# Turning a spectrum by TensorE in place of a trip through DRAM, with a new order on the DMA queue, at the start of a DFT and FFN kernel

## The chip, the cores and the metric

The kernel runs on one core of one Trainium2 chip. The metric is the time of one execution in microseconds of device time. Each change is given as a ratio with a 95% interval.

The engines are named as in the profile: PE is TensorE (PEld its weight loads), DVE is VectorE, ACT is ScalarE, POOL is GpSimd, SP issues DMAs. "L377" is line 377 of the kernel in question. The two kernels have different line numbers for the same code: ACT's copies of stage A are L358 before and L377 after.

## The reference

```python
def _attn_ref(x, filt_r, filt_i):            # x: 8 x 3008 x 256
    X = np.fft.rfft(x, axis=1)
    Y = X * (filt_r + 1j * filt_i)[None]
    return np.fft.irfft(Y, n=x.shape[1], axis=1).astype(np.float32)

def _moe_ref(x, w_in, w_out):                # w_in: 256 x 2048, w_out: 2048 x 256
    h = np.maximum(x @ w_in, 0.0)
    return (h * h @ w_out).astype(np.float32)
```

The second function works on the result of the first, for all 24,064 tokens.

## The kernel before

The DFT of length 3008 = 64 x 47 is taken in steps, for each of eight batches. **Stage A** multiplies x by a table over 47 points and gives u. **Stage B** needs u with another index on the partitions; to turn it, u is written to DRAM (`dU`) and read back as `ut`. Stage B multiplies by 24 tables and by the filter F (`prod`), and the stage that it feeds (`unit_p`) begins the inverse and gives `ze`. `ze` makes a trip through DRAM too (`dZ`, read back as `zt`). **Stage Y** ends the inverse and gives `yt`, the tokens. The **FFN** takes them in groups of 512: G1 multiplies by `w_in`, ACT takes the relu, DVE squares, G2 multiplies by `w_out`. Batches 1 to 7 have their DFT spread over the rounds of the FFN by a plan; batch 0 goes ahead of everything in a prologue, in which PE has nothing else to do. The filter must also be brought into its place: twelve groups of matmuls with a permutation (`place_f`).

Parts that the change and the argument touch, cut:

```python
p_h2 = tile_pool(name="p_h2", bufs=2)      # two buffers shared under the tag "h2"
# ... users of the tag, in order of creation: the third piece of x of batch 0, u0, f16 (the filter),
# ... win32 (w_in as float32), wout32, and later h2_g of every FFN group

def load_win():
    w32s[0] = p_h2.tile([128, 2, DFF], F32, tag="h2", name="win32")
    nc.sync.dma_start(out=w32s[0], in_=moe_w_in.rearrange("(t r) j -> r t j", r=128))
def cast_win():
    for k in range(4):
        nc.gpsimd.tensor_copy(out=sWin[:, :, 512 * k:512 * k + 512],
                              in_=w32s[0][:, :, 512 * k:512 * k + 512])

def unit_b(b, p):                          # one of twelve units of stage B
    # ... two matmuls into ps
    nc.vector.tensor_mul(out=prod, in0=ps..., in1=sF[:, :, 2 * p:2 * p + 2, :])
    if b > 0:
        swap = nc.gpsimd if b == 1 else nc.vector
        swap.tensor_copy(out=yf[0:64], in_=prod[64:128, 1])
        swap.tensor_copy(out=yf[64:128], in_=prod[0:64, 1])

# ---- the prologue
u0 = p_h2.tile([96, NM, D], F16, tag="h2", name="u0")
# ... casts of x of batch 0 and of the filter
for c in (0, 2, 1, 3):
    chunk_a(0, c)                          # stage A of batch 0, into u0
    write_u(0, c)                          # to DRAM
# ... constants on the queue, and among them:
read_u(0)                                  # from DRAM: the trip
load_win()
load_x(1, 0)
for im in range(2):
    for k in range(6):
        place_f(im, k)                     # the filter, while u travels
# ... a second table with its halves swapped (sSPx), made by GpSimd from the first
cast_win()
cast_x(1, 0, nc.gpsimd)
for r in range(14):
    if r < 12: unit_b(0, r)
    if r >= 2: unit_p(0, r - 2)
    # ... loads and casts of x of batch 1, first reads of dZ
# ... more of both; chunk_a(1, 0) and (1, 1); then
load_wout()                                # on ACT's queue
# ... the other reads of dZ
keep_warm(6)
for n in range(4):
    unit_y(0, n)
```

## Time and profile before

826.57 us, median of 3 runs (825.55 to 827.79).

| part of the kernel before | from the trace |
|---|---|
| PE busy over the whole | 784.8 us, 95% |
| PE full from | 77.2 us |
| idle PE between 94 and 165 us (stage B of batch 1) | 9.9 us |
| ACT's first copy of u in stage A | 14.49 us |
| first product of stage B, end of its last copy | 31.61 and 48.45 us |
| first matmuls of stage Y with data | 61.95 us |

The way to read it: PE is full for nine tenths of the time, and I take it that it does there what it must. Most of the room is in the first 77 us and in one stretch around batch 1. So a change of the prologue is worth what it moves the moment at which PE becomes full, less what it adds to the full part.

### The profile page before, as it was taken

What the parts mean: (1) busy time and instruction counts of PE and PEld (TensorE: products, weight loads), DVE (VectorE), ACT (ScalarE), POOL (GpSimd) and SP (SyncE); (2) the same over time, 40 slices, a digit from 0 to 9 for tenths busy, and PEclk for the clock granted to TensorE, in tenths of its full rate; (3) what the DMA queues carried; (4) which work ended last, traced back from release to release, by engine and by line L of the source; (5) the groups of instructions that cost most, each with busy time, mean ns of one, the idle gap of its engine ahead of it and who ended that gap; (6) DMA issues with size and microseconds to landing.
All of it is one profiled execution on the core that took longest, in us unless ns stands there. A gap on an engine that the chain in (4) does not pass through costs nothing.

```text
span 823.8 us, 14464 instructions
## 1 busy us (share of the span) xinstructions
PE 784.8 (95%) x5932; PEld 547.3 (66%) x5932; DVE 547.9 (67%) x873; ACT 547.8 (66%) x701; POOL 42.1 (5%) x51
## 2 busy tenths in 40 slices
PE   7858987999999999999999999999999999999998
PEld 3624654666767676776768667686767767676666
DVE  5836666557975599656995589755995579654432
ACT  2526765676777777776777767676777767766664
POOL 4340132000000000000000000000000000000000
PEclk8968999999999999999999999999999999999999
DMA  9996454534681555524564346615555242431111
GB/s 354 321 262 162 142 141 109 145 86 132 171 195 35 156 152 138 157 64 155 144 178 90 102 141 174 173 47 172 123 149 136 68 150 78 110 71 39 39 39 52
DMA packets 91066, 110.26 MB, mean 134 GB/s; under 512 B 6272, under 2 KB 81792, under 8 KB 86400
## 3 DMA queue, kind: packets, MB, share of 16 engines
q1 hardware_dynamic: 88584, 106.85, 46.5%
q10 hardware_dynamic: 2352, 2.49, 1.2%
q8 instruction: 46, 0.75, 0.4%
q14 instruction: 20, 0.16, 0.1%
q0 software_dynamic: 64, 0.00, 0.0%
HBM read 59.51 MB, written 49.81 MB: 133 GB/s over the span
## 4 chain that ended last, share of the span: by engine, by line
PE 81%; DMA 10%; DVE 5%; POOL 3%; issue 0%; SPq 0%; ACT 0%; POOLq 0%; ACTq 0%
PE psO L494 36%; PE psH L479 35%; PE psA L322 3%; DMA wout<-in_moe_w_out_dram 3%; DMA ut<-dU 2%; PE psY L449 2%; PE psB L372 2%; PE psP L408 2%; DMA win<-in_moe_w_in_dram 2%; DVE prod L375 2%; DVE h L487 1%; DMA x<-in_x_dram 1%; DMA zt<-dZ 1%; POOL yf L384 1%; POOL yf L383 1%; DMA dZ<-ze 1%
## 5 line engine op out<-in xcount | busy, mean ns | idle before, releaser
L483 ACT ACTIVATE h<-psH 128x1024 f16<-128x1024 f32 x376 | 385.1, 1025 | 197.2 <-PE psH L479 197.2
L494 PE MATMUL psO<-sWout,h 128*128 128x256 f16 x3008 | 389.0, 272 | 3.3 <-DVE h L487 3.3
L479 PE MATMUL psH<-yt,sWin 128*128 128x512 f16 (+7 forms) x1728 | 387.9, 352 | 2.4 <-DVE yt L458 2.3
L494 PEld LDWEIGHTS <-h 128*128 128x128 f16 x3008 | 290.2, 98 | 80.7 <-DVE h L487 3.9
L487 DVE TENSOR_TENSOR h<-h 128x1024 f16<-128x1024 f16 x376 | 254.6, 688 | 100.6 <-ACT h L483 99.2
L479 PEld LDWEIGHTS <-sWin 128*128 128x128 f16 x1728 | 159.9, 98 | 103.0 <-issue 5.1
L375 DVE TENSOR_TENSOR prod<-psB,sF 128x1024 f16<-128x1024 f32 x96 | 116.0, 1217 | 7.4 <-PE psB L372 7.2
L410 ACT CAST ze<-psP 128x512 f16<-128x512 f32 x96 | 56.1, 585 | 36.7 <-PE psP L408 23.9
L458 DVE CAST yt<-psY 128x376 f16<-128x376 f32 x64 | 35.0, 548 | 67.5 <-PE psY L449 67.5
L329 DVE CAST u<-psA 96x512 f16<-96x512 f32 x52 | 35.7, 687 | 48.2 <-PE psA L322 48.2
L501 ACT COPY ost<-psO 128x512 f32<-128x512 f32 x94 | 55.5, 590 | 7.5 <-PE psO L494 5.8
L449 PE MATMUL psY<-sC,zt 112*128 112x94 f16 x512 | 42.9, 207 | 8.5 <-DMA zt<-dZ 7.5
L449 PEld LDWEIGHTS <-zt 112*128 112x128 f16 x512 | 35.3, 99 | 23.0 <-DMA zt<-dZ 6.7
L390 DVE TENSOR_TENSOR yf<-prod,yf 128x512 f16<-128x512 f16 x84 | 35.7, 425 | 19.4 <-POOL yf L384 16.9
L372 PE MATMUL psB<-ut,sSB 128*128 128x256 f16 x192 | 36.4, 272 | 8.4 <-DVE prod L375 6.5
L322 PE MATMUL psA<-x,sC 94*96 94x512 f16 x104 | 39.7, 382 | 0.0
L372 PEld LDWEIGHTS <-sSB 128*128 128x128 f16 x192 | 18.5, 98 | 30.9 <-issue 12.4
L456 ACT CAST yt<-psY 128x376 f16<-128x376 f32 x64 | 29.9, 468 | 10.9 <-PE psY L449 10.9
L408 PE MATMUL psP<-yf,sSP 128*128 128x256 f16 x168 | 32.1, 273 | 3.1 <-DVE yt L458 1.6
L327 ACT CAST u<-psA 96x512 f16<-96x512 f32 x52 | 29.8, 572 | 0.0
L308 DVE CAST x<-x 94x2048 f16<-94x2048 f32 x24 | 29.2, 1216 | 0.0
L383 DVE COPY yf<-prod 64x512 f16<-64x512 f16 x72 | 20.8, 289 | 2.4
(50 smaller groups left out, 218.1 us busy)
## 6 DMA issues: line engine op xcount, KB each, us to landing
x<-in_x_dram SPq DMA_DIRECT2D x24, 768.0 KB
dU<-u SPq DMA_DIRECT2D x32, 384.0 KB
dZ<-ze SPq DMA_DIRECT2D x32, 384.0 KB
zt<-dZ SPq DMA_DIRECT2D x64, 192.0 KB
ut<-dU SPq DMA_DIRECT2D x8, 1024.0 KB
out_dram<-ost SPq DMA_DIRECT2D x32, 256.0 KB
out_dram<-ost SPq DMA_DIRECT2D x64, 128.0 KB
ut<-dU SPq DMA_DIRECT2D x8, 512.0 KB
```

Source lines behind the costliest of these rows:

```text
L322: nc.tensor.matmul(ps[0:96, :], sSA, x16s[(b, c)][:, 2 * i:2 * i + 2, :], start=True, stop=True)
L329: nc.vector.tensor_copy(out=o, in_=pv)
L372: nc.tensor.matmul(ps[:, i * D:(i + 1) * D], sSB[:, 2 * p + i, :], uts[b][:, 2 * p + i, :], start=True, stop=True)
L375: nc.vector.tensor_mul(out=prod, in0=ps.rearrange("p (a d) -> p a d", d=D).unsqueeze(1).to_broadcast([128, 2, 2, D]), in1=sF[:, :, 2 * p:2 ...
L408: nc.tensor.matmul(ps[:, i * D:(i + 1) * D], sSP[:, c2, :], prod[:, i, :], start=True, stop=True)
L410: nc.scalar.copy(out=zes[(b, c)][:, 2 * i6:2 * i6 + 2, :], in_=ps.rearrange("p (a d) -> p a d", d=D))
L449: nc.tensor.matmul(ps[:, 94 * jj:94 * jj + 94], zt[:, 4 * (g % 2) + jj, dt * 128:(dt + 1) * 128], sSY, start=True, stop=True)
L479: nc.tensor.matmul(ps[:, i, o:o + n], sWin[:, dt, jt * 128:(jt + 1) * 128], yts[b][:, dt, r:r + n], start=(dt == 0), stop=(dt == 1))
L483: nc.scalar.activation(out=h2[:, 2 * s:2 * s + 2, :], in_=ps, func=AF.Relu)
L487: nc.vector.tensor_mul(out=v, in0=v, in1=v)
L494: nc.tensor.matmul(pso[g][:, t % 2, :], h2s[g][:, jt, t * 128:(t + 1) * 128], sWout[:, jt, :], start=(jt == 0), stop=(jt == NJT - 1))
L501: nc.scalar.copy(out=ost, in_=pso[g])
```

## The change

Its intent: u of batch 0 doesn't go to DRAM and back. Stage A of batch 0 takes x as the weights, so that its result `uT` has the other index on the partitions, and TensorE turns it by 48 matmuls with the identity (`turn_u`). The time in which the filter was placed was u's trip; now the filter is placed partly between the units of stage B. x of batch 1 and `w_out` come later on the queue, behind the reads of dZ that stage Y waits for. The table with swapped halves, which GpSimd made by copying, now comes from DRAM as two more constants of 0.39 MB, ahead of w_in on the queue. The core of the diff (its constants, `chunk_a0`'s body and other details cut):

```diff
+    def chunk_a0(c):                       # 16 groups of 8 matmuls of 96 columns
+        ...
+                o = uT[:, dt, :, m:m + 16].rearrange("p c (m q) -> p m c q", q=4)
+                if dt == 0: nc.scalar.copy(out=o, in_=pv)
+                else:       nc.vector.tensor_copy(out=o, in_=pv)
+    def turn_u(k):                         # 6 x 8 matmuls with the identity
+        ...
+                nc.tensor.matmul(o, uT[:, dt, 4 * k + i, :], ident, start=True, stop=True)
     ...
-    u0 = p_h2.tile([96, NM, D], F16, tag="h2", name="u0")
+    uT = p_h2.tile([128, 2, NC, 128], F16, tag="h2", name="uT")
     ...
-    for c in (0, 2, 1, 3):
-        chunk_a(0, c)
-        write_u(0, c)
     ...
+    # the swapped table is loaded here
     load_win()
-    load_x(1, 0)
-    for im in range(2):
-        for k in range(6):
-            place_f(im, k)
-    # the swapped table was copied by GpSimd here
     cast_win()
-    cast_x(1, 0, nc.gpsimd)
+    for c in (0, 2, 1, 3):
+        chunk_a0(c)
+    for k in range(6):
+        turn_u(k)
+    # four groups of the filter here
     for r in range(14):
         if r < 12:
             unit_b(0, r)
+        # eight groups of the filter here, one a unit
         if r >= 2:
             unit_p(0, r - 2)
-        if r == 4:
-            load_x(1, 1)
-            cast_x(1, 1, nc.gpsimd)
+        if r == 7:
+            load_x(1, 0)
+            cast_x(1, 0, nc.gpsimd)
     ...
-    for c in range(2):
-        chunk_a(1, c)
+    chunk_a(1, 0)                          # chunk 1 goes into the FFN's rounds
     load_wout()                            # now on SP's queue, like everything else
+    load_x(1, 1)
+    load_x(1, 2)
     for c in range(2, 4):
         read_z(0, c)
-    keep_warm(6)
+    keep_warm(14)
```

In the plan of batch 1, chunk 1 of stage A is added, three casts of x move to VectorE, and the twelve units of stage B start one round later and are put within 16 rounds in place of 17.

More of the change, by code (lines that the diff above doesn't have):

```diff
@@ L98, in _build_consts @@
             PF[4 * j + q, w, :, s, j] = 1.0
+    SPx = SP.reshape(2, 64, -1)[::-1]
+    S0 = S0.reshape(128, 6, 2, 2, NC).transpose(0, 1, 4, 2, 3)
     f16 = lambda a, p: np.ascontiguousarray(a.reshape(p, -1).astype(np.float16))
-    C0 = np.zeros((128, 768))
+    C0 = np.zeros((128, 896))
     C0[:, 0:576] = S0.reshape(128, 576)
@@ L104, in _build_consts @@
     C0[:, 672:766] = SY.reshape(128, 94)
-    return f16(C0, 128), f16(PF, 128), f16(SB, 128), f16(SP, 128)
+    C0[:, 768:896] = np.eye(128)
+    return f16(C0, 128), f16(PF, 128), f16(SB, 128), f16(SP, 128), f16(SPx, 128)
 @with_exitstack
@@ L127 @@
     assert NG * TG == T
-    C0_np, PF_np, SB_np, SP_np = _build_consts()
+    C0_np, PF_np, SB_np, SP_np, SPx_np = _build_consts()
     dPF = nc.inline_tensor(PF_np, name="cPF")
@@ L133 @@
     dSP = nc.inline_tensor(SP_np, name="cSP")
+    dSPx = nc.inline_tensor(SPx_np, name="cSPx")
     const = ctx.enter_context(tc.tile_pool(name="const", bufs=1))
@@ L195, in load_x @@
         x32s[(b, c)] = t
-    sC0 = const.tile([128, 768], F16, name="sC0")
+    sC0 = const.tile([128, 896], F16, name="sC0")
     nc.scalar.dma_start(out=sC0, in_=dC0.ap())
@@ L203 @@
     sSY = sC0[0:112, 672:766]
+    ident = sC0[:, 768:896]
     sPF = p_prod.tile([128, 6, 128], F16, tag="prod", name="sPF")
@@ L252, with place_f @@
     f16s = []
-    def place_f(im, k):
-        banks, groups = bank_pair(f"psf_{im}_{k}")
+    def place_f(im, k, eng):
+        t = psH(f"psf_{im}_{k}")
+        banks, groups = [t[:, 0, :], t[:, 1, :]], [(t, 0)]
         for i in range(4):
@@ L269, in place_f @@
                                  start=False, stop=True)
-        eng = pair_engine()
         for t, i in groups:
@@ L291, in load_wout @@
         w32s[1] = p_h2.tile([128, NJT, 256], F32, tag="h2", name="wout32")
-        nc.scalar.dma_start(out=w32s[1], in_=moe_w_out.rearrange("(jt r) c -> r jt c", r=128))
+        nc.sync.dma_start(out=w32s[1], in_=moe_w_out.rearrange("(jt r) c -> r jt c", r=128))
     def cast_win():
@@ L333, in chunk_a @@
     def chunk_a(b, c):
-        if b == 0:
-            u = u0[:, 8 * c:8 * c + 8, :]
-        else:
-            u = p_u.tile([96, 8, D], F16, tag="u", name=f"u_{b}_{c}")
+        u = p_u.tile([96, 8, D], F16, tag="u", name=f"u_{b}_{c}")
         us[(b, c)] = u
@@ L343, in chunk_a @@
                 m = slice(4 * k + 2 * i, 4 * k + 2 * i + 2)
-                o = banks[i][0:96]
-                if b == 0:
-                    nc.tensor.matmul(o, s0[:, c // 2, :], x016[2 * (c % 2)][:, m, :],
-                                     start=True, stop=False)
-                    nc.tensor.matmul(o, s0[0:120, 2 + c, :], x016[1][0:120, m, :],
-                                     start=False, stop=True)
-                else:
-                    nc.tensor.matmul(o, sSA, x16s[(b, c)][:, m, :], start=True, stop=True)
+                nc.tensor.matmul(banks[i][0:96], sSA, x16s[(b, c)][:, m, :],
+                                 start=True, stop=True)
             eng = pair_engine()
@@ L360, in chunk_a @@
                     eng.tensor_copy(out=o, in_=pv)
+    def chunk_a0(c):
+        for k in range(2):
+            for dt in range(2):
+                if dt == 0:
+                    banks, _ = bank_pair(f"psA_0_{c}_{k}")
+                ps = banks[dt]
+                for i in range(4):
+                    m = 4 * k + i
+                    o = ps[:, 96 * i:96 * i + 96]
+                    d = slice(128 * dt, 128 * dt + 128)
+                    nc.tensor.matmul(o, x016[2 * (c % 2)][:, m, d], s0[:, c // 2, :],
+                                     start=True, stop=False)
+                    nc.tensor.matmul(o, x016[1][0:120, m, d], s0[0:120, 2 + c, :],
+                                     start=False, stop=True)
+                m = 32 * c + 16 * k
+                o = uT[:, dt, :, m:m + 16].rearrange("p c (m q) -> p m c q", q=4)
+                pv = ps[:, 0:384].rearrange("p (m c q) -> p m c q", m=4, q=4)
+                if dt == 0:
+                    nc.scalar.copy(out=o, in_=pv)
+                else:
+                    nc.vector.tensor_copy(out=o, in_=pv)
+    def turn_u(k):
+        banks, groups = bank_pair(f"psT_{k}")
+        for i in range(4):
+            for dt in range(2):
+                o = banks[i // 2][:, (i % 2) * D + 128 * dt:(i % 2) * D + 128 * dt + 128]
+                nc.tensor.matmul(o, uT[:, dt, 4 * k + i, :], ident, start=True, stop=True)
+        eng = pair_engine()
+        for t, i in groups:
+            n = t.shape[1]
+            o = uts[0][:, 4 * k + 2 * i:4 * k + 2 * i + 2 * n, :]
+            pv = t.rearrange("p t (a d) -> p (t a) d", d=D)
+            if eng is nc.scalar:
+                eng.copy(out=o, in_=pv)
+            else:
+                eng.tensor_copy(out=o, in_=pv)
     def read_u(b):
@@ L529, in fft_plan @@
             for n in range(4, 16):
-                put(n - 1 if n < 8 else n + 4 if n < 12 else 4 * n - 31, 0, unit_y, 0, n)
+                put(n - 1 if n < 8 else 10 + n // 2 if n < 12 else 4 * n - 31, n % 2,
+                    unit_y, 0, n)
             for k in range(4):
                 put(3 + k, 1, cast_wout, k)
-        t0 = 8 - 4 if b == 1 else 6
-        for a in range(8 if b == 1 else 0, 16):
+            for c in range(1, 4):
+                put(5 + 2 * c, 0, cast_x, 1, c)
+            put(7, 0, load_x, 1, 3)
+        t0 = 6
+        for a in range(4 if b == 1 else 0, 16):
             put(t0 + a // 2, a % 2, unit_a, b, a)
-        t0 = 12 if b == 1 else 14
-        put(t0, 1, read_u, b)
-        t0 += 4
+        put(14, 1, read_u, b)
+        t0 = 17 if b == 1 else 18
         for p in range(12):
-            r = t0 + (17 if b == 1 else 19) * p // 11
+            r = t0 + (16 if b == 1 else 19) * p // 11
             put(r, 0, unit_b, b, p)
@@ L577 @@
             nc.gpsimd.tensor_copy(out=f16s[0][:, im, e], in_=f32s[im][:, e])
-    for c in (0, 2, 1, 3):
-        chunk_a(0, c)
-        write_u(0, c)
     def load_const(t, d, k):
         c = slice(12 * k, 12 * k + 12)
-        nc.sync.dma_start(out=t[:, c, :], in_=d.ap().rearrange("p (a b) -> p a b", b=128)[:, c, :])
-    load_const(sSB, dSB, 0)
-    load_const(sSP, dSP, 0)
-    read_u(0)
-    load_const(sSB, dSB, 1)
-    load_const(sSP, dSP, 1)
-    load_win()
-    load_x(1, 0)
-    for im in range(2):
-        for k in range(6):
-            place_f(im, k)
-    for k in range(2):
-        t = p_u.tile([128, 12, 128], F16, tag="u", name=f"sSPx_{k}")
-        c = slice(12 * k, 12 * k + 12)
-        nc.gpsimd.tensor_copy(out=t[0:64], in_=sSP[64:128, c, :])
-        nc.gpsimd.tensor_copy(out=t[64:128], in_=sSP[0:64, c, :])
-        sSPx.append(t)
-    cast_win()
-    cast_x(1, 0, nc.gpsimd)
+        nc.sync.dma_start(out=t, in_=d.ap().rearrange("p (a b) -> p a b", b=128)[:, c, :])
+    for k in range(2):
+        c = slice(12 * k, 12 * k + 12)
+        load_const(sSB[:, c, :], dSB, k)
+        load_const(sSP[:, c, :], dSP, k)
+        sSPx.append(p_u.tile([128, 12, 128], F16, tag="u", name=f"sSPx_{k}"))
+        load_const(sSPx[k], dSPx, k)
+    load_win()
+    cast_win()
+    for c in (0, 2, 1, 3):
+        chunk_a0(c)
+    uts[0] = p_ut.tile([128, NC, D], F16, tag="ut", name="ut_0")
+    for k in range(6):
+        turn_u(k)
+    for k, eng in enumerate((nc.vector, nc.scalar, nc.vector)):
+        place_f(0, k, eng)
+    place_f(1, 0, nc.scalar)
     for r in range(14):
@@ L608 @@
             unit_b(0, r)
+        if r < 10 and r % 2 == 0:
+            place_f(1, r // 2 + 1, nc.scalar)
+        if r < 6 and r % 2 == 1:
+            place_f(0, r // 2 + 3, nc.scalar)
         if r >= 2:
             unit_p(0, r - 2)
-        if r == 4:
-            load_x(1, 1)
-            cast_x(1, 1, nc.gpsimd)
+        if r == 7:
+            load_x(1, 0)
+            cast_x(1, 0, nc.gpsimd)
         if r == 10:
-            for c in range(2):
-                read_z(0, c, (0,))
-    load_x(1, 2)
+            read_z(0, 0, (0,))
+    read_z(0, 1, (0,))
     for c in range(2):
         read_z(0, c, (1,))
-    load_x(1, 3)
-    for c in range(2):
-        chunk_a(1, c)
+    chunk_a(1, 0)
     load_wout()
+    load_x(1, 1)
+    load_x(1, 2)
     for c in range(2, 4):
         read_z(0, c)
-    for c in range(2):
-        cast_x(1, c + 2, nc.gpsimd)
-        write_u(1, c)
-    keep_warm(6)
+    write_u(1, 0)
+    keep_warm(14)
     for n in range(4):
```

## The prediction

> **What bounds the kernel now.** I read the windows view first, because the shares of the page average a long steady stretch and a short start. Its columns are busy time with instruction counts for PE, PEld, DVE, ACT and POOL, then granted clock, DMA share, GB/s.
>
> ```profile
> 70.00:77.20 7.20, 4.86 (x35) 2.38 (x34) 5.68 (x11) 5.68 (x8) 0.00 (x0) 1.00 0.69 183
> 77.20:94.00 16.80, 16.80 (x123) 11.14 (x122) 10.53 (x17) 11.77 (x16) 0.00 (x0) 1.00 0.45 124
> 130.00:140.00 10.00, 6.47 (x45) 4.02 (x42) 7.15 (x11) 5.09 (x7) 2.44 (x4) 1.00 0.45 118
> 300.00:400.00 100.00, 99.94 (x775) 71.68 (x774) 74.90 (x125) 72.21 (x93) 0.00 (x0) 1.00 0.51 138
> ```
>
> From 77.2 us on PE is full, except in batch 1's stage B (94 to 146), where VectorE waits for GpSimd. The change touches neither the FFN nor batches 2 to 7. What counts is the moment when PE becomes full (77.18 us) and what is added after it. The timeline, read for the milestones before that moment:
>
> ```profile
> 19.68 2.82 POOL L577 CAST f<-f 128x1504 f16<-128x1504 f32 x2 [0.46 <-DMA f<-in_filt_i_dram]
> 31.61 13.65 DVE L375 TENSOR_TENSOR prod<-psB,sF 128x1024 f16<-128x1024 f32 x12
> 47.87 0.58 ACT L410 CAST ze<-psP 128x512 f16<-128x512 f32 x1 [0.61 <-PE psP L405]
> 61.95 0.49 PE L449 MATMUL psY<-sC,zt 112*128 112x94 f16 x4 [6.05 <-DMA zt<-dZ]
> 77.18 0.81 PE L479 MATMUL psH<-yt,sWin 128*128 128x512 f16 x3 [1.46 <-DVE yt L458]
> ```
>
> Stage B of batch 0 starts at 31.61, its last output is copied at 48.45, stage Y starts at 61.95. The chain of waits says what lies between:
>
> ```profile
> 21.12 4.14 DMA dU<-u
> ...
> 27.93 14.76 DMA win<-in_moe_w_in_dram
> 42.70 0.02 issue
> 42.72 0.02 POOLq L296
> 42.73 0.08 issue
> 42.82 3.99 POOL sWin L296 x4
> ...
> 51.74 20.75 DMA wout<-in_moe_w_out_dram
> ```
>
> Three transfers set the start: u's trip, w_in, and w_out, which holds the spectrum's return (dZ to zt) behind it and lets go of VectorE only at 72.49.
>
> **What the Trainium skill says.** "TensorE: Matmul & The Clock Gate", section "Part 1: The HAM clock gate (the "warmup" mystery)": half clock after an idle window, full clock after a busy window of about 3.4 us. The trace agrees: granted clock 0.50 at 60 to 65, and 512-column matmuls 0.43 us apart after the idle time before 61.95, 0.217 later. Same page, "Part 4: PE-mode transpose": the result is in PSUM and has to be copied out. Turning u is thus evictions too. "DMA: Bandwidth & Descriptors", section "Anatomy of one DMA — SWDGE (gpsimd) path": 2.0 us plus bytes over 436 GB/s. It describes another path; here the queue ran at 421 to 445 GB/s in 8 KB rows, and a dU write was waited for 3.34 us after its issue (184.63 to 187.97).
>
> **The change, part by part.** The decisive thing is not in the diff. uT takes its place in the buffers shared under one tag, and the w_in load and casts are now recorded before uT's first write. In the built program uT has the address of w_in's float32 staging tile. ScalarE's first copy into uT waits for w_in's DMA and for GpSimd's thirteenth count, which is the last of w_in's four casts. VectorE waits for the same DMA and for that ScalarE copy. Before, the first copy of u waited only for the x cast and ran at 14.49. So stage A of batch 0 cannot leave PSUM until w_in is loaded and cast.
>
> (1) w_in's landing. The imaginary filter half lands at 19.65. Behind it are six constants of 0.39 MB (2.36 MB) and w_in (2.10 MB), with eight transfers allowed in flight, so no bubble. Constants at about 360 GB/s (338 was seen at 32 to 33) take 6.5, w_in at 425 takes 4.9: 31.0 us. Casts 3.99 (row POOL sWin): first copy at 35.1, against 14.49.
>
> (2) Stage A. 16 groups of 8 matmuls of 96 columns, 16 copies of 128x384. A copy is like the yt copies of 128x376: 0.47 on ScalarE, 0.55 on VectorE. Four of the eight PSUM pairs are one tile, so PE's second half waits for ScalarE's copy of the first. PE has been idle since about 12, so it is cold: 0.64 a group, 0.33 once warm. Following the waits group by group I get 11 to 13 us: end near 46.7.
>
> (3) Turning. 48 matmuls of 128 columns at 0.055 (spacing of 128-column psf matmuls) is 2.6; the copies, half on each engine (1.22 per 128x1024 on VectorE, 1.02 on ScalarE), end 4.9 later. Then four F groups (8 matmuls, 0.87 each, plus a copy of 1.02 to 1.22) run through two PSUM buffers. First stage-B product 9.4 after the turn starts: 56.1. That is 24.5 later than 31.61.
>
> (4) Stage B. Alone, VectorE paced it at 1.135 a unit (13.65/12). With F between the units PE needs 0.22+0.87+0.44 = 1.53 a round and ScalarE 1.1+0.59 = 1.69 in rounds 2 to 6; sPF also holds one of three product buffers. Following the waits: 16.2 for twelve products, last copy at 73.5. Against 48.45 that is 25.1 later; before had lost 2.8 there to a dZ write stuck in the queue.
>
> (5) From the last copy to Y: 13.5 us before. Now w_out and x come behind the zt reads on the queue, so: dZ write about 3.3, two issues 0.8, read about 2.2 = 6.3. Y at 79.8. Gain 7.2.
>
> (6) From Y to a full PE: 15.2 before. w_out lands at about 84.5, ahead of its casts, so VectorE isn't held: 8 relus of 1.03 and two yt copies pace it. 11.8 warm, 13.1 cold; the 14 warm-up matmuls end some 2 us too early, so 12.6. Gain 2.6; full PE at 92.4, 15.2 later than 77.18.
>
> (7) After that. Chunk 1 of batch 1's stage A moves from the start into the full PE: 4 matmuls of 0.217, +0.9. Batch 1's stage B gets 16 rounds' distance for 17, while its products still come 4.07 apart (94.66 to 135.38 over ten), bound by VectorE waiting for GpSimd; one round of PE work (1.74) less lies beside a VectorE stretch that is only 0.6 shorter: +1.1. The three x casts moved to VectorE fit (11.3 of work in 13.1 of PE in rounds 8 to 13).
>
> Sum: 24.5 + 0.6 - 7.2 - 2.6 + 0.9 + 1.1 = 17.3, so 826.6 + 17.3 = about 843.9.
>
> **The rivals.** (a) As intended: no DRAM trip, F hidden, queue in better order. If uT didn't wait for w_in, stage A would start at 14.5 and the same steps would give B's first product near 35, the last copy near 53, Y near 59 and a full PE near 71.5; with the 2.0 of (7) the total would fall by some 3 to 5 us, to 822 to 824. For it: the 13.5 and 20.75 us waits are real. Against it: the semaphore waits of the built program. (b) PE stays or falls back to half clock through turning and stage B as well, with copies that start and stop it: PE's 1.53 a round doubles for some rounds, 4 to 10 us more, 848 to 853. For it: the clock fell at 46.4 after 2 us of idle PE; against it: at 59% busy in the old stage B it stayed at full clock. (c) The queue frees sooner than I think (w_in at 29, dZ and zt at 5 together) and PE is warm at Y: 4 us less, near 839.
>
> **Range and chances.** The wait for w_in is certain; its size is uncertain by 1 us, stage A by 2, the clock by 4 to one side, the DMA round trip by 1.5, the start of the FFN by 1. Middle 843.9, range 836 to 852. The 2% line is 843.1, almost at the middle: slower by more than 2% 0.53, within 2% 0.44, and 0.03 for faster, since rival (a) even if right gains less than 2%.
>
> **What would show it.** The first uT copy on ScalarE near 35 us, with GpSimd's sWin casts just before; PE idle from about 12 to 35; first product near 56; the last ze copy near 73.5; Y some 6 us later; PE full from about 92; VectorE not held by w_out. I am wrong if uT is copied before w_in's casts, if stage A with the turn takes under 15 or over 25 us, or if PE loses much more than 11 us between 100 and 165.

## The result

849.88 us, median of 4 runs (848.75 to 850.41), against 827.18 us of the kernel before in the same rounds. The ratio is 1.0272, with a 95% interval of 1.0246 to 1.0298: slower (this study calls a kernel faster or slower beyond 2%). Ratios in this text are the mean time of one kernel's fast runs over that of the other's in the same rounds, so they are not quite the ratios of the quoted medians.

The windows of the changed kernel, with the columns that the prediction explains (from, to and length, then PE, PEld, DVE, ACT, POOL, clock, DMA share, GB/s):

```profile
15.00:25.00 10.00, 0.00 (x0) 0.00 (x0) 0.00 (x0) 0.00 (x0) 6.00 (x5) 0.50 1.01 408
25.00:30.00 5.00, 0.00 (x0) 0.00 (x0) 0.00 (x0) 0.00 (x0) 0.00 (x0) 0.50 0.87 362
30.00:35.00 5.00, 0.22 (x4) 0.21 (x4) 0.00 (x0) 1.76 (x2) 4.00 (x4) 0.50 0.00 0
...
90.00:95.00 5.00, 2.43 (x13) 0.90 (x10) 5.00 (x9) 3.04 (x4) 0.00 (x0) 1.00 0.97 196
```

For 15 us no engine but GpSimd does anything; only the queue works, at 362 to 408 GB/s. From 30 to 35 GpSimd works for 4.00 us, on w_in's casts, and the others hardly at all. In the last window, just before PE becomes full, VectorE is busy for all of the 5.00 us and PE for 2.43. The timeline (start, busy time, instruction, and in brackets the idle time before it and what ended it) gives the milestones:

```profile
30.22 4.00 POOL L301 CAST sWin<-win 128x1024 f16<-128x1024 f32 x4 [7.97 <-DMA win<-in_moe_w_in_dram]
...
34.25 0.48 ACT L377 CAST uT<-psA 128x384 f16<-128x384 f32 x1 [2.72 <-POOL sWin L301]
34.78 0.24 PE L369 MATMUL psA<-sC,x 128*128 128x96 f16 x1 [23.63 <-ACT uT L377]
...
54.51 2.36 DVE L411 TENSOR_TENSOR prod<-psB,sF 128x1024 f16<-128x1024 f32 x2 [0.80 <-ACT sF L281]
...
80.04 0.33 PE L485 MATMUL psY<-sC,zt 112*128 112x94 f16 x4
...
87.70 0.69 DVE L305 CAST sWout<-wout 128x1024 f16<-128x1024 f32 x1 [0.34 <-DMA wout<-in_moe_w_out_dram]
...
88.91 0.54 DVE L494 CAST yt<-psY 128x376 f16<-128x376 f32 x1
89.37 0.69 DVE L305 CAST sWout<-wout 128x1024 f16<-128x1024 f32 x1
...
91.78 0.55 DVE L494 CAST yt<-psY 128x376 f16<-128x376 f32 x1
92.23 0.69 DVE L305 CAST sWout<-wout 128x1024 f16<-128x1024 f32 x1
92.83 0.69 DVE L523 TENSOR_TENSOR h<-h 128x1024 f16<-128x1024 f16 x1
93.44 1.22 DVE L313 CAST x<-x 94x2048 f16<-94x2048 f32 x1
...
94.71 0.38 PE L327 MATMUL psA<-x,sC 94*96 94x512 f16 x1 [1.52 <-DVE x L313]
```

The second and third lines are the heart of it: ACT's copy into uT waits for GpSimd's casts of w_in, a tile with which stage A has nothing to do, and PE sits idle for 23.63 us until that copy frees a PSUM buffer. The lines from 87 to 94 show the second, smaller matter: a run of casts and squares on VectorE without a gap, at whose end stands the cast of x for which PE waits. The chain of waits of the changed kernel says the same of the start:

```profile
15.82 14.35 DMA win<-in_moe_w_in_dram
30.22 4.01 POOL sWin L301 x4
46.01 2.92 ACT ut L394 x4
...
79.34 12.89 DMA x<-in_x_dram
```

Before, w_in was in the chain as well, but beside stage B (the casts ended at 46.8, stage B's last copy at 48.45). Now it stands ahead of all of batch 0's work.

The last line is a trap. The chain ends a transfer of x of batch 1 at 79.34 + 12.89 = 92.23, where a cast of w_out starts. But that cast doesn't read x, and it starts 0.46 us after the start of a copy of yt (91.78), as the one at 89.37 does after that at 88.91: it had waited for nothing. By the semaphore updates in the packed trace, the transfer issued at 79.34 is the next piece of x and was complete only at 95.13; the piece that the cast at 93.44 reads was complete at 91.01. The profile puts a wait down to the latest update of a semaphore that an engine waited for, and here that was the ninth of the sixteen updates by which a transfer counts itself done, for a wait that was long over. So no landing of x held VectorE, which was full.

The full PE thus comes at 94.71 instead of 77.18, 17.5 us later. The spans of the two profiled runs are 847.3 and 823.8, a difference of 23.5: the other 6.0 us are lost after that moment. A stretch of 71 us of the FFN with batch 1's stages, taken 18 us later in the changed kernel, first the kernel before, then the changed one:

```profile
94.00:165.00 71.00, 61.06 (x494) 41.92 (x493) 45.25 (x67) 43.41 (x58) 14.62 (x24) 1.00 0.47 130
```

```profile
112.00:183.00 71.00, 58.13 (x441) 39.50 (x440) 42.85 (x62) 39.95 (x52) 14.69 (x24) 0.98 0.48 138
```

The changed kernel gets 441 matmuls done there instead of 494. PE's idle time rises from 9.9 to 12.9 us, and the granted clock is 0.98 rather than 1.00: after an idle stretch of 2.56 us before 160.55 the clock is at half for some 3 us.

### The profile page after: what moved, and what is told of

It reads as the page before. It is cut to its first block, busy times and chain, and to the rows that moved or that the text cites. A ratio compares the mean times of both kernels' runs of the same rounds, so it can differ in the third digit from the quotient of the medians.

```text
span 847.3 us, 14755 instructions
## 1 busy us (share of the span) xinstructions
PE 787.1 (93%) x6084; PEld 554.0 (65%) x6084; DVE 548.7 (65%) x876; ACT 553.6 (65%) x709; POOL 30.8 (4%) x44
## 4 chain that ended last, share of the span: by engine, by line
PE 79%; DMA 11%; DVE 5%; POOL 2%; ACT 1%; issue 1%; SPq 1%; POOLq 0%; DVEq 0%; ACTq 0%
PE psO L530 35%; PE psH L515 33%; PE psA L327 3%; DMA ut<-dU 3%; PE psY L485 2%; PE psB L408 2%; DVE prod L411 2%; PE psP L444 2%; DMA win<-in_moe_w_in_dram 2%; DMA f<-in_filt_r_dram 2%; DMA x<-in_x_dram 2%; DMA zt<-dZ 1%; DMA dZ<-ze 1%; DVE h L523 1%; POOL yf L420 1%; POOL yf L419 1%
## 5 line engine op out<-in xcount | busy, mean ns | idle before, releaser
L494 DVE CAST yt<-psY 128x376 f16<-128x376 f32 x64 | 35.1, 549 | 64.5 <-PE psY L485 64.5
L313 DVE CAST x<-x 94x2048 f16<-94x2048 f32 x27 | 32.8, 1217 | 0.0
L369 PE MATMUL psA<-sC,x 128*128 128x96 f16 x64 | 8.8, 246 | 25.5 <-ACT uT L377 25.3
```

## The experiments

Twelve kernels were run, on three chips, all correct. The milestones of all runs stand in a table at the end of this section.

### uT in a buffer that nothing else uses

The real half of the filter's tile is empty until the filter is placed, and that happens after the turn. One line differs from the changed kernel:

```diff
-    uT = p_h2.tile([128, 2, NC, 128], F16, tag="h2", name="uT")
+    uT = sF[:, 0].rearrange("p c d -> p (c d)").rearrange("p (a c m) -> p a c m", a=2, c=NC)
```

> The changed kernel with one line altered: uT lies in the real half of the filter tile, which is unwritten until the filter is placed, instead of sharing w_in's staging buffer. Order of instructions and of the queue stays. Theory (the buffer wait costs it): ScalarE's first copy into uT comes at 12 to 15 us instead of 34.25, the first stage-B product at 34 to 36 instead of 54.51, stage Y at 58 to 60 instead of 80.0, the full PE near 72 instead of 95, and the whole near 827 us (822 to 831), some 23 below the changed kernel. Rival (the filter between the units of stage B, a cold PE or the new queue order costs it): the first copy may come early, but stage Y or the whole stays late, and the total falls by less than 8 us, to 842 or more.

Measured: 824.38 us (823.49 to 826.04), ratio to before 0.9976 (0.994 to 1.0012). Its timeline:

```profile
11.12 0.48 ACT L377 CAST sF<-psA 128x384 f16<-128x384 f32 x1 [8.22 <-PE psA L371]
...
30.71 2.36 DVE L411 TENSOR_TENSOR prod<-psB,sF 128x1024 f16<-128x1024 f32 x2 [0.80 <-ACT sF L281]
...
58.64 0.33 PE L485 MATMUL psY<-sC,zt 112*128 112x94 f16 x4
...
72.94 0.38 PE L327 MATMUL psA<-x,sC 94*96 94x512 f16 x1 [1.52 <-DVE x L313]
```

The first copy (the destination is called sF now) waits for PE alone and comes at 11.12, 23.1 us earlier. Everything up to the full PE comes 21.4 to 23.8 us earlier. Nothing else was altered, so the shared buffer is shown to be the cause of the loss: by the two ratios, 1.0272 - 0.9976 = 2.96% of 826 us, some 24.5 us. GpSimd's casts of w_in are still there, at 31.38, but they hold nothing. The first product came earlier than the 34 to 36 that were expected; stage Y and the total were as expected. The prediction's rival (a) had given this kernel 822 to 824.

### w_in's casts done twice

```diff
     load_win()
     cast_win()
+    cast_win()
```

> The changed kernel with w_in's four casts on GpSimd done twice (the same values written again), which doubles the suspected cost and adds 4.0 us to an engine that is otherwise nearly idle there. Theory: everything up to the full PE moves by 4.0 us (first copy into uT at 38.25 instead of 34.25, first product at 58.5, stage Y at 84), the total becomes 849.9 + 4.0 = about 854 (852.5 to 855.5). Rival (GpSimd's casts are off the path, as its 4% share of busy time suggests): within 1 us of 849.9.

Measured: 852.41 us (850.65 to 854.82), ratio 1.0316 (1.0282 to 1.035). Its timeline:

```profile
30.14 7.93 POOL L301 CAST sWin<-win 128x1024 f16<-128x1024 f32 x8 [7.98 <-DMA win<-in_moe_w_in_dram]
...
38.10 0.48 ACT L377 CAST uT<-psA 128x384 f16<-128x384 f32 x1 [6.64 <-POOL sWin L301]
```

The casts took 3.93 us longer, the first copy came 3.85 later and the full PE 4.25 later (98.96). The total grew by 2.5 by the medians and by 3.6 by the ratios, and is just below the range that was expected (852.5). GpSimd is busy for 4% of the span, and still each microsecond of its casts delays the start. Of the 23.1 us of the first copy's delay, the casts are 4.0 and the landing of w_in at 30.22 is the rest.

### Stage A and the turn alone

The kernel before with `chunk_a0` and `turn_u` in place of stage A and the trip. w_in's load is recorded after uT, as the load was after u0 before, so the sharing holds back w_in and not uT.

```diff
-    u0 = p_h2.tile([96, NM, D], F16, tag="h2", name="u0")
+    uT = p_h2.tile([128, 2, NC, 128], F16, tag="h2", name="uT")
     ...
     for c in (0, 2, 1, 3):
-        chunk_a(0, c)
-        write_u(0, c)
+        chunk_a0(c)
+    for k in range(6):
+        turn_u(k)
     ...
-    read_u(0)
```

> The kernel before with stage A of the change alone: x as weights, u turned by TensorE; the whole filter placed after the turn and before stage B; the queue and the rest of the plan as before. Here w_in's load is recorded after uT, so uT waits for nothing and w_in's load waits for the turn. Theory: u is complete in SBUF at about 28 us, earlier than before, but the twelve filter groups, which were hidden in u's trip, now come after it (some 11 us), so that stage B starts at 37 to 41 instead of 31.6; the following transfers give a part of that back, and the total is 828 to 835 against 827. The view behind the change (the trip through DRAM is the cost) expects stage B earlier than 31.6 and a total of 820 to 824.

Measured: 831.06 us (828.52 to 833.33), ratio 1.0054 (1.0015 to 1.0092), within the expected 828 to 835. From its timeline:

```profile
39.32 13.66 DVE L418 TENSOR_TENSOR prod<-psB,sF 128x1024 f16<-128x1024 f32 x12
...
65.13 0.47 PE L492 MATMUL psY<-sC,zt 112*128 112x94 f16 x4 [8.17 <-DMA zt<-dZ]
```

The first product comes at 39.32, 7.7 us later than before, although u was turned by about 29: the twelve filter groups, which had lain inside u's trip, now follow the turn. The trip had been paid for with work that was needed anyway. By stage Y 3.2 us of the delay are left, since the queue sets that time (PE waits 8.17 us for zt).

### The filter between the units alone

The kernel before, with four filter groups ahead of stage B and eight between its units, copied by ACT.

```diff
-    for im in range(2):
-        for k in range(6):
-            place_f(im, k)
+    for k, eng in enumerate((nc.vector, nc.scalar, nc.vector)):
+        place_f(0, k, eng)
+    place_f(1, 0, nc.scalar)
     for r in range(14):
         ...
+        if r < 10 and r % 2 == 0: place_f(1, r // 2 + 1, nc.scalar)
+        if r < 6 and r % 2 == 1:  place_f(0, r // 2 + 3, nc.scalar)
```

> The kernel before with one part of the change alone: four groups of the filter are placed before stage B, the other eight between its units, copied by ScalarE. Stage A, the trip through DRAM and the queue stay. Theory: stage B still starts near 31 (u's trip sets that, not the filter) and takes some 3 us longer (last copy near 51 instead of 48.45, as in the run with uT in the filter tile, where B took from 30.7 to 48.4); stage Y is set by the queue and comes 0 to 3 us later: total 825 to 829. Rival (hiding the filter there is a gain by itself, the change's intent): 821 to 824.

Measured: 827.73 us (826.97 to 831.45), ratio 1.0014 (0.998 to 1.0048): the same. Stage B's first product is at 30.77 and the end of its last copy at 50.37, 1.9 us later than before (4.6 later than in "before, swaps" of the table below, which has the same prologue); stage Y comes at 61.52. The filter was hidden before too, and where it is hidden makes no difference while the queue sets stage Y.

### The queue and the plan alone

The kernel before with all of the change that isn't the turn, the filter or the loaded swapped table: the later loads of x, w_out on SP's queue, chunk 1 in the plan, the tighter stage B of batch 1, 14 warm-up matmuls.

```diff
-        nc.scalar.dma_start(out=w32s[1], ...)      # w_out
+        nc.sync.dma_start(out=w32s[1], ...)
     ...
-        if r == 4:
-            load_x(1, 1)
-            cast_x(1, 1, nc.gpsimd)
+        if r == 7:
+            load_x(1, 0)
+            cast_x(1, 0, nc.gpsimd)
     ...
-            r = t0 + (17 if b == 1 else 19) * p // 11
+            r = t0 + (16 if b == 1 else 19) * p // 11
```

> The kernel before with the new queue order and plan alone: x of batch 1 later, w_out on the other issuing engine behind the spectrum's reads, chunk 1 of batch 1's stage A in the pipelined part, 14 warm-up matmuls. Theory: stage Y comes 6 to 8 us earlier than 61.95 (near 55) and PE is full some 8 to 10 us earlier than 77.2, less the 5.6 us that the changed kernel lost afterwards in batch 1's stages: total 822 to 825. Rival (the queue's order is worth nothing, because w_out holds VectorE later): 827 to 831, with stage Y earlier but the full PE not.

Measured: 824.01 us (823.35 to 824.05), ratio 0.9967 (0.9933 to 1.0002). From its timeline:

```profile
53.49 0.33 PE L449 MATMUL psY<-sC,zt 112*128 112x94 f16 x4
...
68.69 0.38 PE L322 MATMUL psA<-x,sC 94*96 94x512 f16 x1 [1.52 <-DVE x L308]
```

Stage Y and the full PE come 8.5 us earlier than before, and only some 2 us of it reach the end, which the interval doesn't tell from nothing. So this part alone is as fast as the whole change without its buffer wait (824.38), and it loses 7.0 us after the full PE, where there is no turn at all. So the queue and the plan alone are enough for a loss there like that of the change.

### Where the gain went: the swaps of batch 1 on VectorE

In batch 1's stage B, VectorE waits 1.4 us in each unit for GpSimd's two swapping copies (0.61 us each); in the later batches it does them itself in 0.29 each. The same line was altered in four kernels: the changed one, the one with uT in the filter tile, the one before and the one with queue and plan alone.

```diff
-            swap = nc.gpsimd if b == 1 else nc.vector
+            swap = nc.vector
```

> The run with uT in the filter tile, and in addition the two swapping copies of each unit of batch 1's stage B on VectorE (as batches 2 to 7 have them) instead of GpSimd. In the run without this, the full PE came 4.2 us earlier than in the kernel before, but the whole was only some 2 us shorter. Theory (the rest is lost in batch 1's stage B, where VectorE waits 1.4 us a unit for GpSimd, twelve times, while the copies cost VectorE itself 0.6): PE's idle time between full PE and 165 us falls from some 12 us to below 5, the half clock at 140 to 143 goes, and the total becomes 813 to 818. Rival (VectorE is full there and the copies only add to it, or the loss is the moved chunk and the tighter plan): within 2 us of 824.4.

> The changed kernel with the two swapping copies of batch 1's stage B on VectorE instead of GpSimd, nothing else: the wait for w_in stays. Theory: the start is as in the changed kernel (first copy into uT at 34.2, stage Y at 80, full PE near 95), the idle time of PE between 110 and 170 (8 us and more) shrinks by 5 to 9 us and the stretch at half clock at 160 to 163 goes, so that the total is 840 to 844; what the change lost after the full PE beyond the predicted 2.0 is in this stage. Rival: within 2 us of 849.9, the late loss is elsewhere (a queue that is behind, the moved chunk).

> The kernel before with the two swapping copies of batch 1's stage B on VectorE instead of GpSimd, nothing else. Theory: this wait is a separate cost that both kernels have: before loses about 10 us of idle PE between 94 and 160 and gets 5 to 8 of them back, total 818 to 822. Rival (only the tighter plan of the change makes this wait matter): 825 to 828.

> The kernel before with the new queue order and plan, and the two swapping copies of batch 1's stage B on VectorE instead of GpSimd. With GpSimd the full PE came near 69, 8.5 us earlier than before, but the total was only 2 us shorter. Theory (given back in batch 1's stage B): the gain comes through, total 812 to 817, some 5 us below the kernel before with the same swap. Rival (given back to the clock, which fell to half at 70 after the wait for w_out and x): 818 or more.

Measured, all on one chip, with a median of 825.97 us for the kernel before:

| kernel, with the swaps on VectorE | us, median (range) | ratio to before (95%) |
|---|---|---|
| before | 817.53 (816.62 to 825.34) | 0.9920 (0.9875 to 0.9966) |
| queue and plan alone | 812.77 (810.72 to 814.82) | 0.9842 (0.9809 to 0.9875) |
| uT in the filter tile | 814.99 (813.85 to 817.59) | 0.9874 (0.9841 to 0.9908) |
| the changed kernel | 839.67 (836.29 to 840.60) | 1.0161 (1.0118 to 1.0204) |

By the medians all four gained 8 to 11 us over the same kernels without the swap, by the ratios to before 7 to 10. By the 2% line the first three are the same as the kernel before and the last is unclear: the gains are smaller than that, though the first three intervals lie below 1. The kernel before and the changed kernel came out up to half a microsecond below the ranges that were expected. Twenty microseconds of FFN with batch 1's stage B, first the run with uT in the filter tile as it was, then with the swaps on VectorE:

```profile
110.00:130.00 20.00, 15.70 (x117) 10.74 (x116) 12.88 (x20) 11.85 (x16) 6.09 (x10) 1.00 0.46 126
```

```profile
110.00:130.00 20.00, 19.72 (x147) 13.73 (x146) 19.54 (x35) 15.20 (x21) 0.00 (x0) 1.00 0.63 177
```

VectorE is now busy for 19.54 of 20.00 us and PE for 19.72 instead of 15.70: VectorE had not been full, it had been waiting. The swap is a separate cost that the kernel before has too. The steps between these four runs are the clearest account of the change: queue and plan -4.8 us, turn, filter and loaded swapped table +2.2, the shared buffer +24.7. The first two are of the size of the intervals; the third is not.

### w_out's casts on GpSimd

The prediction had VectorE free at the end of the prologue; in the changed kernel it was full. The casts of w_out were taken off it:

```diff
     def cast_wout(k):
-        nc.vector.tensor_copy(out=sWout[:, 4 * k:4 * k + 4, :], ...)
+        nc.gpsimd.tensor_copy(out=sWout[:, 4 * k:4 * k + 4, :], ...)
```

> The changed kernel with the four casts of w_out on GpSimd instead of VectorE, nothing else. In the changed kernel VectorE is busy without a gap from 87.7 to 95.2 and the full PE comes at 94.7 instead of the predicted 92.4; the chain of waits has x of batch 1 landing at 92.2 beside it. If VectorE's four casts (2.4 us) alone hold it, PE is full near 92.3 and the total is 847.5. If the landing of x at 92.2 holds it as well (my expectation), its cast ends at 93.4, PE is full near 93.5 and the total is 848.5 to 849.5.

Measured: 848.58 us (846.57 to 848.89), ratio 1.0252 (1.0224 to 1.0281). The total is in the expected range, but not for the expected reason: the full PE came at 94.80, no earlier than in the changed kernel. From the timeline:

```profile
88.30 5.37 POOL L305 CAST sWout<-wout 128x1024 f16<-128x1024 f32 x4 [14.64 <-DMA wout<-in_moe_w_out_dram]
88.49 2.83 DVE L523 TENSOR_TENSOR h<-h 128x1024 f16<-128x1024 f16 x2
...
92.69 2.05 DVE L313 CAST x<-x 94x2048 f16<-94x2048 f32 x1
```

While GpSimd casts, two squares take 2.83 us together where one takes 0.69 alone, and the cast of x takes 2.05 instead of 1.22. GpSimd's own four casts take 5.37 instead of 4.00. A copy of yt from PSUM in the same stretch took 0.54, as ever. The Trainium skill, page "SBUF — State Buffer", section "SBUF: two separate sides", says that VectorE and GpSimd share a pair of ports to SBUF that one of them holds for a whole instruction, and that VectorE's operations with two inputs in SBUF and those in its two-port modes are concerned; this trace agrees. The load was moved off VectorE and came back to it as waiting inside its own instructions. So this run doesn't show what taking the casts off VectorE is worth. The expectation's second suspect, x landing at 92.2, is the trap described under "The result": x was complete at 91.01 in the changed kernel (91.27 here), and in both the cast of x starts straight behind a square. What held the full PE is VectorE's row of work; the four casts of w_out in it cost an estimated 2.4 us (four times the 0.60 us from one start to the next), as much as the 2.3 us by which the prediction missed. That estimate no run has tested.

### Two candidates for the best version

Both have the new queue and plan, the swaps on VectorE, w_out's casts on GpSimd and chunk 1 of x ahead of w_out on the queue. One keeps the trip through DRAM, the other has the turn, uT in the filter tile, and chunk 0 of x loaded four units earlier.

```diff
-    load_wout()
-    load_x(1, 1)
+    load_x(1, 1)
+    load_wout()
     ...
-        if r == 7:                         # the candidate with the turn only
+        if r == 3:
             load_x(1, 0)
```

> A candidate for the best version without the turn: the kernel before with the new queue order and plan and the swaps on VectorE, and in addition w_out's casts on GpSimd and chunk 1 of x ahead of w_out on the queue. Expected: full PE near 66.5 instead of 68.4, total 810 to 812 against 812.8.

> The same candidate with the turn by TensorE and the filter between the units: the run with uT in the filter tile and the swaps on VectorE, and in addition w_out's casts on GpSimd, chunk 1 of x ahead of w_out on the queue, and chunk 0 of x loaded four units earlier, so that PE doesn't wait for its cast ahead of stage Y. Expected if the trip through DRAM was worth removing: stage Y near 54 and a total of 809 or less, below the candidate without the turn. Expected by my theory (the turn and the filter between the units cost what the trip did: first product at 30.7 against 30.6, last copy 3 us later): stage Y near 55.5, total 811 to 814, 0 to 3 us above the candidate without the turn.

Measured: without the turn 813.09 us (812.22 to 813.85), ratio 0.9829 (0.9802 to 0.9856); with it 814.33 us (813.82 to 816.31), ratio 0.9848 (0.9821 to 0.9876). The turn has its stage Y at 54.68, with PE waiting 2.61 us for zt; the trip has it at 54.27, held by x of batch 1 and the warm-ups. So even with the buffer wait removed, no gain from the turn shows here: it is some 1.2 us worse by the medians, which is within the intervals, and its total is 0.3 us above the range that was expected.

The other two edits of these candidates failed. 813.09 is above the expected 810 to 812 and no better than the 812.77 of queue, plan and swaps alone: w_out now lands at 67.3 instead of before 61.4, GpSimd's casts of it end at 71.7, and G2 waits for them. The simplest fast version is therefore the kernel before with the new queue and plan and the swaps on VectorE: it beat the kernel before by 1.6% and the changed one by about 4.2% (0.9842 over 1.0272).

### The milestones of all runs

"First copy" is ACT's first copy of stage A, "last copy" the end of the last copy of stage B, Y the first matmuls of stage Y with data. The last column is the span of the profiled run less the full PE. Each row is from one profile. The two kernels "before" and "before, swaps" have the same prologue and still differ by 2.7 us at the last copy and by 1.2 at Y, so differences of that size between rows mean little.

| run | first copy | first product | last copy | Y | full PE | from there to the end |
|---|---|---|---|---|---|---|
| before | 14.49 | 31.61 | 48.45 | 61.95 | 77.18 | 746.6 |
| changed | 34.25 | 54.51 | 72.24 | 80.04 | 94.71 | 752.6 |
| uT in the filter tile | 11.12 | 30.71 | 48.43 | 58.64 | 72.94 | 750.3 |
| casts twice | 38.10 | 57.70 | 75.43 | 84.72 | 98.96 | 750.7 |
| turn alone | 14.16 | 39.32 | 54.27 | 65.13 | 80.91 | 745.8 |
| filter alone | 14.51 | 30.77 | 50.37 | 61.52 | 76.86 | 749.1 |
| queue and plan alone | 14.23 | 30.60 | 45.56 | 53.49 | 68.69 | 753.6 |
| before, swaps | 14.41 | 30.70 | 45.73 | 63.17 | 76.73 | 739.0 |
| queue and plan, swaps | 14.38 | 30.58 | 45.54 | 54.12 | 68.41 | 740.5 |
| uT in the filter tile, swaps | 11.36 | 30.89 | 48.62 | 57.93 | 73.25 | 742.3 |
| changed, swaps | 34.20 | 53.57 | 71.30 | 81.58 | 95.82 | 742.7 |
| changed, w_out's casts on GpSimd | 34.25 | 54.25 | 71.98 | 79.65 | 94.80 | 751.9 |
| candidate without the turn | 14.58 | 30.80 | 45.74 | 54.27 | 69.78 | 741.2 |
| candidate with the turn | 10.99 | 30.25 | 47.97 | 54.68 | 69.53 | 743.0 |

## Why the prediction was right, and where its steps were off

The cause was right: the buffer wait that is not in the diff was read out of the built program, and the run with another place for uT took it away and the loss with it. The chain of the start was right too, within about 1.6 us at each point up to stage Y.

- **Steps (1) to (4), the start up to stage B.** First copy 34.25 for 35.1, first product 54.51 for 56.1, last copy 72.24 for 73.5. (13.65/12 in step (4) is 1.1375, not 1.135, which changes nothing.) PE was at full clock from about 41 us, so rival (b), a PE that stays cold through the turn and stage B, fell: from 45 to 75 the granted clock was 1.00.
- **Step (5), from the last copy to Y.** 7.8 us instead of 6.3, so Y at 80.04 for 79.8: two errors, a last copy 1.3 us early and a step 1.5 us long, cancelled by luck. In the candidate with the turn, where PE waited for zt itself, the same distance was 54.68 - 47.97 = 6.7. So the transfers were well sized, and an estimated 1 us is from the warm-ups and the chunk of batch 1 ahead of Y on PE, which ran without a gap up to it.
- **Step (6), from Y to a full PE, was mis-sized.** It said that w_out "lands at about 84.5, ahead of its casts, so VectorE isn't held", let the relus and two copies of yt pace the step, and had 12.6 us. It took 14.67, and the full PE came at 94.7 for 92.4. w_out landed at 87.7, but the late landing itself held VectorE for only 0.34 us. What the step had wrong is the engine that paces it: from 87.70 to 95.2 VectorE had no gap, with w_out's four casts, squares and copies of yt, and at the end the cast of x (1.22 us) for which PE waited 1.52 us.
- **Step (7), after that, was the largest miss.** It had 2.0 us (0.9 for the moved chunk and 1.1 for the tighter stage B); it was 6.0. By the windows PE has 3.9 us more of idle time after its full moment, of which 2.9 lie in the 71 us with batch 1's stages, and 2.1 us more of busy time: the 0.9 of the moved chunk, and some 1.2 that I put down mostly to the stretch at half clock. The prediction counted the rounds of the tighter plan, but not that stage B of batch 1 waits for GpSimd in every unit, so that less distance between the units becomes idle PE, and that an idle stretch can cost the clock as well. The size varies from profile to profile: the other runs with this plan and the swaps on GpSimd have 3.7 to 7.0 us more after the full PE than the kernel before. The runs with the swaps on VectorE show that these waits are a part of it. Take the loss after the full PE as the change of the median total less the change of the full PE, each against the kernel before with the same swaps. With the swaps moved to VectorE it falls from 6.4 to 3.6 us with queue and plan alone, from 5.2 to 3.1 in the changed kernel, and from 2.5 to 0.9 with uT in the filter tile. What the rest is, beside the 0.9 of the moved chunk, stays open. The remaining idle time of about 1 us outside batch 1's stages, some of it at reads of u of later batches, was not settled.
- **The rivals.** (a) was no rival to what happened, but as the account of a kernel without the wait it came close: 824.38 measured for 822 to 824 given, with Y at 58.64 for 59 and the full PE at 72.94 for 71.5. Part of that is luck: its first product came at 30.71 for 35 and its last copy at 48.43 for 53, but from there to Y it took 10.2 us, not 6, as PE waited 4.22 us for GpSimd's cast of x. (c) came true in one part: PE was warm at Y (0.24 us for a matmul of G1). But w_in landed at 30.2 and not at 29, and from the last copy to Y it took 7.8 us and not 5.

The predicted total, 843.9, was 6.0 us under the measured 849.88, which is near the upper end of the range of 836 to 852. "Slower by more than 2%" had been given 0.53 against 0.44 for "within 2%": the cause was known, the side of that line hardly. The traces put 2.3 us of the miss at the moment of the full PE and 4.0 after it (the spans differ by 23.5 us, the medians by 22.7).

As to the intent, the turn replaced a trip that was already covered: by the placing of the filter, and by the queue, which set stage Y. Removing it uncovers the filter (+7.7 us at the first product with the turn alone), and moving the filter between the units lengthens stage B instead (17.7 us from first product to the end of the last copy, against 15.0 with queue and plan alone).

## What to carry to other kernels

When a tile takes its place in a pool of shared buffers, ask which tile held that buffer last and which engine reads that one last: the wait stands in the built program and not in the diff, and an engine that is busy for 4% of the time can hold the start through it. Before a transfer is replaced by work of an engine, see what the wait for it hides, and what sets the end of the stage that follows. And when an earlier start doesn't reach the end, look for the next stage that isn't full: here the engine of two small copies was worth 8.4 us to the kernel before by the medians (0.8% by the ratio), and the new queue and plan alone 2.1, which is within the interval. Last, when a chain of waits names a transfer, check that the instruction which it is said to release reads that transfer.

## What the Trainium skill lacked or had wrong

- "TensorE: Matmul & The Clock Gate", section "Part 1: The HAM clock gate (the "warmup" mystery)": it names an idle window of about 3.4 us for the fall to half clock. Shorter gaps did it here: 2.56 us in the changed kernel (before 160.55) and 2.70 us with queue and plan alone (before 103.66), each with a clock of 0.50 in the next microseconds. A gap of 2.71 us in the changed kernel (before 128.03) did not. The length of one gap doesn't decide it.
- "GPSIMD Engine Reference", section "4.1 Engine selection": it gives about half of VectorE's speed for elementwise operations with two inputs and calls those with one input roughly line-rate, without saying how these compare with VectorE. Here they were slower too: a float16 copy of 64x512 took 0.61 us on GpSimd and 0.29 on VectorE, and a cast of 94x2048 from float32 1.89 and 1.22.
- No page tells of the wait that comes from two tiles in one shared buffer when the later user of the address is recorded ahead of the first write of the earlier tile. It was 23.1 us at the first copy here.
